# q and k brought in with their rows as columns, so that TensorE does not turn them

## The chip, the cores and the metric

The kernel runs on one core of one Trainium2 chip. Its time is the device time of one execution in microseconds (us); the median of several runs is compared. The profile shows one execution, engine by engine: PE is TensorE, PEld its weight loads, DVE is VectorE, ACT is ScalarE, POOL is GpSimd, and SPq is the queue of SyncE, which issues nearly all DMAs. What the host does to the inputs before the launch is not in this time.

## The reference, cut to what matters

```python
# q, k, v: (4 batches, 8 heads, 576 rows, 64), f32
scores = scale * np.matmul(q, k.transpose(0, 1, 3, 2))
thresh = np.max(scores, axis=-1, keepdims=True) - tau
scores = np.where(scores >= thresh, scores, -1000000000.0)
attn = softmax(scores)
x = attn @ v                     # then the heads side by side: 2304 x 512
x = np.maximum(x @ w_in, 0.0) ** 2 @ w_out          # 512 -> 2048 -> 512
# top-1 of 8 experts by x @ w_gate: relu(x @ w1[e]) @ w2[e], times two gates
```

## The kernel before

The work is a graph of tasks, each with an engine, a planned cost, the buffers that it reads and writes, and a key (a due time). `Graph.schedule` (L108) plays the graph through with the planned costs and fixes one order per engine; the program is written in that order, and every engine and the SP queue run theirs strictly in order. So the order comes from planned costs, and the times from the chip.

Attention goes by pairs of heads, 16 pairs (`pr`), four to a batch. A pair has 9 chunks of 128 query rows (`t_chunk`): scores on PE (L653; L688 for the first two chunks), row maximum on DVE (L656), threshold and exponential on ACT (L664, L659), masking with a sum on DVE (L668), normalizing on POOL or ACT (L679, L711), five transposes on PE (L733), copies out of PSUM on ACT (L744, L750) and DVE (L753), and then the product with v (`t_av`, L794 in the first batch, L776 later). While batch b is in attention, PE also does the first dense layer of batch b-1 (`t_h`, L873: 32 units of 12 matmuls for a batch). After the attention come the rest of that layer, the second layer (L991) and the experts (L1255, L1305).

Products keep f32 accuracy by splitting an operand into a rounded part (`hi`, type fp32r) and the rest (`lo`). Each pair is prepared during the pair before it (`pair_prep`):

- `t_load` brings k, q and v from HBM into `kraw`, `qraw`, `vraw`, one buffer each. For k and q, partition p gets rows 4p to 4p+3 of both heads in pieces of 64 numbers (256 bytes): a main DMA of 128x8x64 (L532) and a tail for the last 64 rows (L526).
- `t_qk` turns each of them, in two parts: 3 and 2 transposes on PE (L576) into a PSUM bank of the pool `pM`; then ACT makes `hi` from that bank (L584 for k, L586 for q, which is scaled through `qsc`) and DVE makes `lo` from the bank and `hi` (L592, L594). The results are `xk` and `xq`, with 2 x 64 channels of the two heads on the partitions and 576 rows as columns.
- `t_op` copies pieces of `xk` and `xq` within SBUF to the operands `opA` and `opB` of the scores (L608, L611, L614), and `t_diag` a piece of `xq` to `xd` (L629), on the SP queue.

The pool `pM` has two banks, and L576, the products with v and the units of `t_h` share them. `w_in` is fetched and converted during the attention too (`t_w`, DVE L850 to L854).

## Time and profile before

| | |
|---|---|
| median of 3 runs | 1034.44 us (1034.28 to 1034.68) |
| the profiled execution | 1033.64 us, its span from first to last instruction 1031.9 us |
| PE busy | 991.9 us, 96% of the span |
| PEld, DVE, ACT, POOL busy | 85%, 67%, 62%, 33% |
| DMA | 167.85 MB, of 165437 packets 60367 under 512 B |
| mean granted TensorE clock | 0.990 of full speed |

Busy shares are averages over stages with different limits, so the stages have to be read one by one. Matmuls are pipelined, and the busy time of a short group of them reaches past the start of the next instruction; the price of a group within a full stream is better read from its start to the next start. The difference of 1.7 us between the profiled execution and its span lies outside of the instructions.

### The profile page before, as it was taken

The page shows a single profiled execution, that of the slowest core. Times are in us where ns is not written, and L with a number is a line of the kernel's source. Part 1 is how long each engine was busy: PE and PEld are TensorE (multiplying, and loading weights), DVE is VectorE, ACT ScalarE, POOL GpSimd, SP SyncE. Part 2 cuts the span into 40 slices and gives each one's busy share as a digit, 9 for nine tenths or more (in the row PEclk, how much of TensorE's full clock was granted, in tenths as well). Part 3 has the DMA queues.
Part 4 walks back from the last instruction along what each step waited for, and adds up shares of the span by engine and source line. Part 5 has one row for each costly group of instructions (what it writes and reads, how often), then busy time and mean ns, then how long its engine had stood idle before and what let it go on. Part 6 is the DMA issues. An engine that isn't in the chain of part 4 may idle for free.

```text
span 1031.9 us, 19062 instructions
## 1 busy us (share of the span) xinstructions
PE 991.9 (96%) x6276; PEld 875.1 (85%) x6276; DVE 696.2 (67%) x1579; ACT 640.0 (62%) x1331; POOL 344.1 (33%) x660
## 2 busy tenths in 40 slices
PE   6999889999999999999999999999999999999995
PEld 5656589899999999999998888888889999889894
DVE  4668899987878778975972444434687667767730
ACT  5878667776666667765744444444666667867730
POOL 1234698775666566563000000010112211111200
PEclk9999989999999999999999999999999999999998
DMA  6556566654455544633882444433768868877700
GB/s 153 123 148 157 144 172 181 158 139 119 125 128 144 143 126 121 185 104 114 255 252 78 115 114 118 120 107 83 212 196 278 278 205 280 285 273 260 266 20 24
DMA packets 165437, 167.85 MB, mean 163 GB/s; under 512 B 60367, under 2 KB 126159, under 8 KB 165330
## 3 DMA queue, kind: packets, MB, share of 16 engines
q1 hardware_dynamic: 161090, 156.03, 52.8%
q0 software_dynamic: 4096, 10.52, 3.1%
q8 instruction: 52, 0.85, 0.3%
q14 instruction: 55, 0.45, 0.1%
q10 hardware_dynamic: 144, 0.00, 0.0%
HBM read 110.72 MB, written 29.56 MB: 136 GB/s over the span
## 4 chain that ended last, share of the span: by engine, by line
PE 74%; DVE 7%; issue 6%; DMA 6%; POOL 4%; ACT 2%; SPq 1%; DVEq 0%; POOLq 0%; ACTq 0%
PE bank L991 18%; PE bank L873 16%; PE bank L1305 8%; PE bank L1255 8%; PE bank L653 6%; PE bank L733 5%; PE bank L776 4%; PE bank L794 3%; DMA out_dram<-memf 2%; PE bank L1275 2%; DVE memf L656 2%; DVE memf L668 1%; PE bank L1110 1%; DVE memr L753 1%; POOL memf L679 1%
## 5 line engine op out<-in xcount | busy, mean ns | idle before, releaser
L873 PE MATMUL bank<-memr,w 128*128 128x288 f32 x1536 | 226.4, 298 | 1.5 <-DVE memr L594 1.4
L873 PEld LDWEIGHTS bank<-memr,w 128*128 128x128 f32 x1536 | 209.6, 189 | 3.6 <-DVE memr L594 3.2
L991 PE MATMUL bank<-w,memr 128*128 128x512 f32 x648 | 157.4, 394 | 0.0
L991 PEld LDWEIGHTS bank<-w,memr 128*128 128x128 f32 x648 | 119.1, 188 | 23.4
L668 DVE SCALAR_TENSOR_TENSOR memf<-bank,memf 128x576 f32<-128x576 f32 x144 | 116.0, 813 | 26.0 <-ACT memf L659 22.6
L656 DVE TENSOR_REDUCE memf<-bank 128x1 f32<-128x576 f32 x144 | 106.7, 750 | 23.5 <-PE bank L653 20.4
L653 PE MATMUL bank<-memr 128*128 128x288 f32 x600 | 110.9, 313 | 9.8 <-DVE memf L668 8.1
L733 PE MATMUL bank<-ident,memf 128*128 128x128 f32 x720 | 106.1, 278 | 9.2 <-ACT ptf L744 4.2
L679 POOL TENSOR_SCALAR memf<-memf 128x576 f32<-128x576 f32 x128 | 99.8, 782 | 31.2 <-DVE memf L676 21.3
L659 ACT ACTIVATE memf<-bank,memf 128x576 f32<-128x576 f32 x144 | 104.3, 732 | 0.0
L1096 POOL DMA_INDIRECT lst<-memf x18 | 17.8, 989 | 258.6 <-DVE memf L1082 112.8
L733 PEld LDWEIGHTS bank<-ident,memf 128*128 128x128 f32 x720 | 82.7, 142 | 21.1 <-issue 5.3
L653 PEld LDWEIGHTS bank<-memr 128*128 128x128 f32 x600 | 86.3, 192 | 15.5 <-DVE memf L668 11.1
L750 ACT ACTIVATE memr<-bank 128x640 fp32r<-128x640 f32 (+1 forms) x120 | 76.7, 649 | 25.6 <-PE bank L733 22.4
L1255 PE MATMUL bank<-memr,w 128*128 128x256 f32 x564 | 88.9, 283 | 0.7 <-DVE memr L1265 0.6
L976 DVE TENSOR_TENSOR memr<-memf,memr 128x512 fp32r<-128x512 f32 x72 | 48.3, 700 | 61.1 <-ACT memf L973 59.5
L1240 DVE TENSOR_TENSOR w<-memf,w 128x512 fp32r<-128x512 f32 x114 | 74.0, 687 | 16.0 <-ACT w L1237 12.5
L673 POOL TENSOR_SCALAR memf<-memf 128x1 f32<-128x1 f32 x144 | 31.2, 216 | 149.4 <-DVE memf L668 134.7
L753 DVE TENSOR_TENSOR memr<-bank,memr 128x512 fp32r<-128x512 f32 (+1 forms) x120 | 74.6, 629 | 9.2 <-ACT memr L750 7.7
L1255 PEld LDWEIGHTS bank<-memr,w 128*128 128x128 f32 x564 | 77.4, 191 | 2.0 <-DVE memr L1265 1.1
L1305 PE MATMUL bank<-memr 128*128 128x512 f32 x306 | 77.3, 393 | 0.0
L664 ACT ACTIVATE memf<-memf,ntau 128x1 f32<-128x1 f32 x144 | 41.5, 293 | 52.3 <-DVE memf L656 42.5
(145 smaller groups left out, 1743.8 us busy)
## 6 DMA issues: line engine op xcount, KB each, us to landing
memf<-in_moe_w_dram SPq DMA_DIRECT2D x104, 512.0 KB
r_scr<-memf SPq DMA_DIRECT2D x128, 144.0 KB
memf<-r_scr SPq DMA_DIRECT2D x36, 512.0 KB
memr<-memr SPq DMA_DIRECT2D x64, 144.0 KB
memr<-memr SPq DMA_DIRECT2D x64, 128.0 KB
memr<-memr SPq DMA_DIRECT2D x32, 256.0 KB
memf<-in_moe_w_in_dram SPq DMA_DIRECT2D x16, 512.0 KB
memf<-in_moe_w_out_dram SPq DMA_DIRECT2D x16, 512.0 KB
```

The source lines that it names most:

```text
L653: nc.tensor.matmul(s.t[:, hf, :HALF], qo, ko[:, halves[hf]], start=(i == 0), stop=(i == len(ops) - 1))
L656: nc.vector.tensor_reduce(nm.t, s.t[:, :, :HALF], axis=AX.XY, op=ALU.max, negate=True)
L659: nc.scalar.activation(p.t[:, :S].rearrange("p (a n) -> p a n", a=2), s.t[:, :, :HALF], AF.Exp, bias=nm.t)
L668: nc.vector.scalar_tensor_tensor(p3, s.t[:, :, :HALF], th.t, p3, op0=ALU.is_ge, op1=ALU.mult, accum_out=sm.t)
L679: nc.gpsimd.tensor_scalar(p.t[:, :S], p.t[:, :S], sm.t, 1.0, op0=ALU.mult, op1=ALU.mult)
L733: nc.tensor.transpose(ps.t[:, j], p.t[:, j * P : (j + 1) * P], ident)
L750: nc.scalar.activation(pt.t[:, :NQ, off : off + w], ps.t[:, :, c0 : c0 + w], AF.Copy)
L753: nc.vector.tensor_tensor(pt.t[:, NQ:, off : off + w], ps.t[:, : NQ - 1, c0 : c0 + w], pt.t[:, : NQ - 1, off : off + w].bitcast(F32), op=A ...
L873: nc.tensor.matmul(ps.t[:, :HALF], wv[:, a, kc], xT.t[:, x, kc, half], start=(i == 0), stop=(i == len(seq) - 1),)
L991: nc.tensor.matmul(ps.t, s.t[:, fc], wob[fc].t[:, x], start=(fc == 0 and i == 0), stop=(fc == NFC - 1 and i == 2))
L1255: nc.tensor.matmul(ps.t[:, :256], w1b[kc][fc // 4].t[:, a, (fc % 4) * P : (fc % 4 + 1) * P], x2.t[:, x, kc], start=(i == 0), stop=(i == 11))
L1305: nc.tensor.matmul(ps.t, hT.t[:, a, fc, u * P : (u + 1) * P], w2b[fc].t[:, x], start=(fc == 0 and i == 0), stop=(fc == 7 and i == 2))
```

## The change

`kernel()` lays q and k out on the host as (batch, pair, 2 x 64 channels, 576 rows), with the rows in the order in which the transposes left them. A load of k or q is then one DMA of 128 partitions x 2304 bytes, without a tail; `t_qk` has no PE task, takes no bank of `pM`, and makes `hi` and `lo` of all 576 columns by one ACT and one DVE instruction that read `kraw` or `qraw` in SBUF. Removed per pair: 10 transposes on PE, 2 of 4 instructions on ACT, 2 of 4 on DVE, 2 DMAs. A raw buffer, which became free after the transposes, becomes free after `lo`.

```diff
-        ("kraw", 1, [P, NQ, 2, D]), ("qraw", 1, [P, NQ, 2, D]), ("vraw", 1, [P, 2, NQ, D]),
+        ("kraw", 1, [P, S]), ("qraw", 1, [P, S]), ("vraw", 1, [P, 2, NQ, D]),
...
-        hs = {"k": k, "q": q, "v": v}[nm][b, 2 * hp : 2 * hp + 2]
+        if nm != "v":
+            src = {"k": k, "q": q}[nm][b, hp]
+            dma(lambda: nc.sync.dma_start(buf.t, src), P * S * 4, [], [buf], key)
+            return
...
-    def t_qk(pr, nm, part, key):
+    def t_qk(pr, nm, key):
...
-        def tp():
-            o = 0
-            for c in cs:
-                sz = QSZ[c]
-                nc.tensor.transpose(
-                    ps.t[:, o : o + sz], raw.t[:sz, c].rearrange("p a d -> p (a d)"), ident[:sz, :sz]
-                )
-                o += sz
...
-                nc.scalar.activation(X, ps.t[:, :n], AF.Copy, scale=qsc)
+                nc.scalar.activation(xy.t[:, 0], raw.t, AF.Copy, scale=qsc)
...
-                nc.vector.scalar_tensor_tensor(Y, ps.t[:, :n], qsc, X, op0=ALU.mult, op1=ALU.subtract)
...
-        g.add("PE", 0.109 * len(cs), tp, [(raw, 0), (raw, 1)] + ([(raw, 2)] if 4 in cs else []), [ps], key, hold=[xy])
-        g.add("ACT", c_act(n, True, nm == "q"), hi, [ps], [(xy, 0, part)], key - 1)
-        g.add("DVE", c_dve(n), lo, [ps, (xy, 0, part)], [(xy, 1, part)], key - 1)
+                nc.vector.scalar_tensor_tensor(xy.t[:, 1], raw.t, qsc, X, op0=ALU.mult, op1=ALU.subtract)
+
+        g.add("ACT", c_act(S, False, nm == "q"), hi, [raw], [(xy, 0)], key - 1)
+        g.add("DVE", c_dve(S), lo, [raw, (xy, 0)], [(xy, 1)], key - 1)
...
+    turned = {"k": order, "q": np.roll(order, 64)}
...
+        if name in turned:
+            a = np.swapaxes(a, 2, 3)[..., turned[name]].reshape(4, 4, 128, 576)
```

The order is planned anew. On PE, in the third batch, where pair 10 (counted from 0) is prepared during the chunks of pair 9, these rows stood before (bank_1_68 and bank_1_69 are the two banks of `pM`, bank_2_77 and bank_2_78 hold scores, w_80 and w_81 are parts of `w_in`):

```order
L776 MATMUL bank_1_68<-memr 128x320 x9
L576 MATMUL bank_1_69<-ident,memf 128x128 x3
L733 MATMUL bank_2_73<-ident,memf 128x128 x5
L653 MATMUL bank_2_78<-memr 128x288 x6
L576 MATMUL bank_1_68<-ident,memf 128x128
L576 MATMUL bank_1_68<-ident,memf 128x64
L576 MATMUL bank_1_69<-ident,memf 128x64
L576 MATMUL bank_1_69<-ident,memf 128x128 x2
L653 MATMUL bank_2_77<-memr 128x288 x4
L733 MATMUL bank_2_73<-ident,memf 128x128 x5
L576 MATMUL bank_1_68<-ident,memf 128x128 x2
L873 MATMUL bank_1_69<-memr,w_81 128x288 x12
```

In the changed kernel the same place on PE reads as follows, with new line numbers (L752 is the old L776, L629 the old L653, L709 the old L733, L849 the old L873):

```order
L752 MATMUL bank_1_68<-memr 128x320 x9
L629 MATMUL bank_2_78<-memr 128x288 x6
L709 MATMUL bank_2_73<-ident,memf 128x128 x5
L849 MATMUL bank_1_69<-memr,w_81 128x288 x12
L629 MATMUL bank_2_77<-memr 128x288 x4
L849 MATMUL bank_1_68<-memr,w_81 128x288 x4
L709 MATMUL bank_2_73<-ident,memf 128x128 x5
L849 MATMUL bank_1_68<-memr,w_81 128x288 x8
L752 MATMUL bank_1_69<-memr 128x256 x9
```

The ten transposes are gone, the units of `t_h` have moved up between the chunks, and nothing has come in the place of the transposes.

On the SP queue, at the start of the program, these rows stood before:

```order
L532 DMA memf<-in_k_dram 128x8x64
L526 DMA memf<-in_k_dram 64x2x64
L532 DMA memf<-in_q_dram 128x8x64
L526 DMA memf<-in_q_dram 64x2x64
L530 DMA memf<-in_v_dram 128x2x256
L524 DMA memf<-in_v_dram 64x2x64
L947 DMA lst<-memf 128x340
L532 DMA memf<-in_k_dram 128x8x64
L608 DMA memr<-memr 64x576 x2
L614 DMA memr<-memr 64x512
L611 DMA memr<-memr 64x2x512
L614 DMA memr<-memr 64x512
```

In the changed kernel the SP queue starts with these rows (L522 is the load of k or q, L584, L587 and L590 are the old L608, L611 and L614, L605 is the old L629):

```order
L522 DMA memf<-in_k_dram 128x576
L522 DMA memf<-in_q_dram 128x576
L530 DMA memf<-in_v_dram 128x2x256
L527 DMA memf<-in_v_dram 64x2x64
L923 DMA lst<-memf 128x340
L927 DMA y_scr<-memf 1x513
L584 DMA memr<-memr 64x576 x3
L587 DMA memr<-memr 64x2x512
L590 DMA memr<-memr 64x512 x2
L584 DMA memr<-memr 64x576
```

The load of q is now the second DMA instead of the third, and the next pair's load of k no longer stands ahead of the first pair's copies; it follows behind all of them.

## Rows read from the trace of the kernel before

**Rows 1.** Busy time by stage: PE, PEld, DVE, ACT, POOL, then clock, DMA share, GB/s.

```profile
15.00:105.00 90.00, 80.91 (x453) 55.38 (x453) 65.76 (x152) 72.18 (x149) 29.26 (x56) 1.00 0.59 142
105.00:190.00 85.00, 77.85 (x500) 66.14 (x500) 75.93 (x167) 60.12 (x128) 64.66 (x119) 0.94 0.59 156
190.00:427.00 237.00, 234.33 (x1789) 226.94 (x1788) 193.53 (x441) 163.37 (x358) 151.21 (x340) 1.00 0.54 139
427.00:960.00 533.00, 531.95 (x3149) 468.24 (x3148) 332.66 (x767) 314.05 (x637) 88.15 (x124) 1.00 0.60 186
```

**Rows 2.** Busy time by stage, L576 alone: PE, PEld, clock, DMA share, GB/s.

```profile
0.00:15.00 15.00, 3.69 (x13) 2.28 (x13) 1.00 0.75 176
15.00:105.00 90.00, 7.71 (x42) 4.98 (x42) 1.00 0.59 142
105.00:190.00 85.00, 4.56 (x23) 2.74 (x23) 0.94 0.59 156
190.00:568.00 378.00, 15.07 (x82) 9.89 (x82) 1.00 0.54 148
```

**Rows 3.** Timeline of PE from 278.1 us: start, duration, instruction, idle before.

```profile
278.16 0.49 PE L576 MATMUL bank<-ident,memf 128*128 128x128 f32 x3
278.48 0.71 PE L733 MATMUL bank<-ident,memf 128*128 128x128 f32 x5
...
279.83 0.90 PE L576 MATMUL bank<-ident,memf 128*128 128x128 f32 x5
280.49 0.77 PE L653 MATMUL bank<-memr 128*128 128x288 f32 x4
...
281.65 0.38 PE L576 MATMUL bank<-ident,memf 128*128 128x128 f32 x2
282.24 0.40 PE L873 MATMUL bank<-memr,w 128*128 128x288 f32 x1 [0.21 <-DVE memr L594]
...
307.71 0.49 PE L576 MATMUL bank<-ident,memf 128*128 128x128 f32 x3
```

**Rows 4.** Groups by line: xcount, busy us, mean ns, idle before.

```profile
L594 DVE SCALAR_TENSOR_TENSOR memr<-bank,qsc,memr 128x320 fp32r<-128x320 f32 (+1 forms) x32 | 16.3, 511 | 1.5 <-ACT memr L586 1.4
L586 ACT ACTIVATE memr<-bank,qsc 128x320 fp32r<-128x320 f32 (+1 forms) x32 | 15.7, 500 | 2.7 <-PE bank L576 1.5 <-DVE memf L668 0.4 <-DMA memf<-in_moe_w_out_dram 0.2
L592 DVE TENSOR_TENSOR memr<-bank,memr 128x384 fp32r<-128x384 f32 (+1 forms) x32 | 14.2, 451 | 3.0 <-ACT memr L584 2.5
L584 ACT ACTIVATE memr<-bank 128x384 fp32r<-128x384 f32 (+1 forms) x32 | 13.0, 414 | 8.6 <-PE bank L576 7.7 <-DVE memr L592 0.7
L711 ACT ACTIVATE memf<-memf 128x576 f32<-128x576 f32 x16 | 12.2, 779 | 0.4 <-DVE memf L676 0.4
L976 DVE TENSOR_TENSOR memr<-memf,memr 128x512 fp32r<-128x512 f32 x72 | 48.3, 700 | 61.1 <-ACT memf L973 59.5 <-DMA memf<-in_moe_w_dram 1.6
```

**Rows 5.** Chain that ended last, first 16 us: start, duration, what.

```profile
0.73 3.98 DMA memf<-in_k_dram
...
6.90 0.99 PE bank L576 x3
...
8.48 0.95 DVE memr L594 x2
...
9.45 0.62 SPq L611
...
10.12 4.83 DMA memr<-memr
```

**Rows 6.** Waits of the SP queue: us in total, times, longest.

```profile
SPq L532 <- PE bank L576: 35.9, 15, 6.0
```

**Rows 7.** Line L576, PE's idle time before it by releaser: us, times.

```profile
  DMA memf<-in_k_dram: 4.9, 1
```

**Rows 8.** Busy time by stretch, columns as in Rows 1.

```profile
103.00:112.00 9.00, 6.39 (x28) 4.47 (x28) 8.16 (x18) 5.96 (x13) 5.53 (x9) 0.81 0.53 136
130.00:139.00 9.00, 5.79 (x28) 4.49 (x28) 8.96 (x20) 5.84 (x14) 8.76 (x15) 0.75 0.65 168
```

More of the change, by code (lines that the diff above doesn't have):

```diff
@@ L555, in t_v @@
             g.add("POOL", 0.1 + NQ * D * 0.0024, lo, src + [(buf, j, 0)], [(buf, j, 1)], key)
-    def t_qk(pr, nm, part, key):
+    def t_qk(pr, nm, key):
         raw = raws[pr, nm]
-        xs = xks if nm == "k" else xqs
-        if pr not in xs:
-            xs[pr] = new("x" + nm, pr)
-        xy = xs[pr]
-        if nm == "k":
-            cs, n0 = ((0, 1, 2), 0) if part == 0 else ((3, 4), 384)
-        else:
-            cs, n0 = ((4, 0, 1), 0) if part == 0 else ((2, 3), 320)
-        n = sum(QSZ[c] for c in cs)
-        ps = Buf(pM, f"tp{pr}{nm}{part}")
-        def tp():
-            o = 0
-            for c in cs:
-                sz = QSZ[c]
-                nc.tensor.transpose(
-                    ps.t[:, o : o + sz], raw.t[:sz, c].rearrange("p a d -> p (a d)"), ident[:sz, :sz]
-                )
-                o += sz
+        xy = (xks if nm == "k" else xqs)[pr] = new("x" + nm, pr)
         def hi():
-            X = xy.t[:, 0, n0 : n0 + n]
             if nm == "k":
-                nc.scalar.activation(X, ps.t[:, :n], AF.Copy)
+                nc.scalar.activation(xy.t[:, 0], raw.t, AF.Copy)
             else:
-                nc.scalar.activation(X, ps.t[:, :n], AF.Copy, scale=qsc)
+                nc.scalar.activation(xy.t[:, 0], raw.t, AF.Copy, scale=qsc)
         def lo():
-            X = xy.t[:, 0, n0 : n0 + n].bitcast(F32)
-            Y = xy.t[:, 1, n0 : n0 + n]
+            X = xy.t[:, 0].bitcast(F32)
             if nm == "k":
-                nc.vector.tensor_tensor(Y, ps.t[:, :n], X, op=ALU.subtract)
+                nc.vector.tensor_tensor(xy.t[:, 1], raw.t, X, op=ALU.subtract)
             else:
-                nc.vector.scalar_tensor_tensor(Y, ps.t[:, :n], qsc, X, op0=ALU.mult, op1=ALU.subtract)
-        g.add("PE", 0.109 * len(cs), tp, [(raw, 0), (raw, 1)] + ([(raw, 2)] if 4 in cs else []), [ps], key, hold=[xy])
-        g.add("ACT", c_act(n, True, nm == "q"), hi, [ps], [(xy, 0, part)], key - 1)
-        g.add("DVE", c_dve(n), lo, [ps, (xy, 0, part)], [(xy, 1, part)], key - 1)
+                nc.vector.scalar_tensor_tensor(xy.t[:, 1], raw.t, qsc, X, op0=ALU.mult, op1=ALU.subtract)
+        g.add("ACT", c_act(S, False, nm == "q"), hi, [raw], [(xy, 0)], key - 1)
+        g.add("DVE", c_dve(S), lo, [raw, (xy, 0)], [(xy, 1)], key - 1)
     def t_op(pr, j, key):
@@ L614, in turn_q @@
             nc.sync.dma_start(q3(slice(64, 128))[:, 1 - x], xq.t[rows, x, 64:].bitcast(F32))
-        parts = lambda xy, *xs: [(xy, x, p) for x in xs for p in range(2)]
+        parts = lambda xy, *xs: [(xy, x) for x in xs]
         for x in range(2):
@@ L629, in t_diag @@
             dma(lambda r=r: nc.sync.dma_start(xd.t[r, :, r].bitcast(F32), xq.t[r, :, 0:64].bitcast(F32)),
-                32768, [(xq, x, 0) for x in range(2)], [(xd, j)], key)
+                32768, [(xq, x) for x in range(2)], [(xd, j)], key)
     def t_chunk(n, key):
@@ L692, in mm @@
                     i += 1
-            rd = [(xk, x, p) for x in range(2) for p in range(2)] + [(xq, x, 0 if c < 2 else 1) for x in range(2)]
+            rd = [(y, x) for y in (xk, xq) for x in range(2)]
             g.add("PE", c_pe(HALF) * 8, mm, rd, [s], key)
         elif hd == 2:
-            rd = [(xk, x, p) for x in range(2) for p in range(2)] + [(xds[pr], j) for j in range(2)]
+            rd = [(xk, x) for x in range(2)] + [(xds[pr], j) for j in range(2)]
             g.add("PE", c_pe(HALF) * 6, mm, rd, [s], key + K("scores", pr))
@@ L1324, in pair_prep @@
         for nm in "kq":
-            for part in range(2):
-                t_qk(pr, nm, part, key)
+            t_qk(pr, nm, key)
         for j in range(2):
@@ L1423, in put @@
         args.append(nc.dram_tensor(name, a.shape, mybir.dt.from_np(a.dtype), kind="ExternalInput").ap())
+    p = np.arange(512)
+    order = np.concatenate([4 * (p % 128) + p // 128, np.arange(512, 576)])
+    turned = {"k": order, "q": np.roll(order, 64)}
     for name in _INS:
-        a = np.ascontiguousarray(inputs[name])
+        a = inputs[name]
+        if name in turned:
+            a = np.swapaxes(a, 2, 3)[..., turned[name]].reshape(4, 4, 128, 576)
+        a = np.ascontiguousarray(a)
         if a.ndim == 0:
```

13 lines of the change are left out of this document (4 added, 9 removed).

## The prediction

> **What bounds the kernel now.** PE is by far the busiest engine of the page (96% of the span, the table above), so the first question is in which stages its work is what time is made of. The busy times by stage [rows 1] tell. From 190 us on PE is full: 234.33 of 237 us while attention runs beside the first dense layer, and 531.95 of 533 after that. DVE, the next engine, has 193.53 of the 237, so PE alone sets the pace there, and what PE does not do is saved one for one. Before 190 us it is different. From 15 to 105 us (the first batch, no dense work beside it) PE has 80.91 of 90 and ACT 72.18: mostly PE, with pauses for the chain of a chunk. From 105 to 190 us DVE has 75.93 of 85, PE 77.85, and the granted clock is 0.94: two engines close to full, and neither covers the other.
>
> Then I read L576, the transposes of q and k, alone by stage [rows 2]: 13 before 15 us, 42, 23, and 82 from 190 us on, together the 160 of 16 pairs. Last, the timeline of PE in the full stretch [rows 3], for the price of one preparation; there a preparation comes every 307.71 - 278.16 = 29.55 us.
>
> **The change part by part.**
>
> *Transposes from 190 us on.* The busy times of L576 [rows 2] reach past the start of the next instruction, so I price a preparation from start to next start [rows 3]: 278.48 - 278.16 = 0.32, 280.49 - 279.83 = 0.66, 282.24 - 281.65 = 0.59, together 1.57 us for ten transposes. The last holds a wait of 0.21 us for DVE, which frees the bank of `pM`; it goes too, since q and k take no bank any more. 82 transposes are 8.2 preparations: 8.2 x 1.57 = 12.9 us. Nothing comes in their place on PE, as the order shows. I take all of it, because PE is full before and after; the lower bound is 10, if every preparation leaves a new pause of about 0.35 us.
>
> *Transposes from 15 to 105 us.* 42 of them, at most 4.2 x 1.57 = 6.6 us; nothing, if the chain of a chunk sets the pace throughout. PE's 90% is nearer to the first, but some transposes also fill pauses: I take 4.0.
>
> *From 105 to 190 us.* 23 transposes, at most 3.6 us. Here DVE counts as much as PE, so its saving is worked out. The makers of `lo` cost (16.3 + 14.2) / 16 = 1.91 us per pair now, those of `hi` on ACT (15.7 + 13.0) / 16 = 1.79 [rows 4]. The new ones read SBUF, and q and k have no such row. Nearest on ACT is L711, 576 columns out of SBUF with a scale, 779 ns; nearest on DVE is L976, 512 columns out of SBUF, 700 ns, so 788 for 576. Two each make 1.56 on ACT and 1.58 on DVE, 0.23 and 0.33 less per pair. (Were one instruction as dear as the two that it replaces, the difference would be nothing.) Three pairs in this stretch give DVE 1.0 us. With a little of the PE work I take 1.5, between 0 and 3.6. From 190 us on the savings of ACT and DVE are worth nothing, because PE's work covers them.
>
> *The start.* The chain of the first 16 us [rows 5] runs: load of k (from 0.73, 3.98 long), transposes and parts of k, transposes of q (6.90), `lo` of q ready at 8.48 + 0.95 = 9.43, copies to the operands, the last of which lands at 10.12 + 4.83 = 14.95, scores. In the changed kernel the load of q is SP's second DMA, issued one issue time (some 0.65, from 9.45 to 10.12) after the first, at 1.4. If it takes the 3.98 of k, q is there at 5.4; `hi` takes 0.78, `lo` 0.79, ready at 7.0 instead of 9.43: 2.4 us. The copies behind it are as many and as large, and the next pair's load of k no longer runs beside them. Bounds: 1.0, if the loads get in each other's way and q lands 1.4 later; 4, if loads in rows of 2304 bytes are shorter by 1.6. No row of this kernel shows q or k loaded in whole rows.
>
> The Trainium skill, DMA: Bandwidth & Descriptors, Specifications, puts the smallest transfer at line rate at 512 B; the pieces grow from 256 to 2304 bytes, so by it the load shortens, the start gives up to 4 us, and the total would be 1012.0 instead of the 1013.6 below.
>
> *DMA and SP.* 32 DMAs fewer on the SP queue I count as nothing, since PE has no idle time in the full stretch that they could end. A raw buffer becomes free after `lo` instead of after the transposes, 9.43 - 7.89 = 1.5 us later for q [rows 5]. The next load waits for the buffer on SP already: 35.9 us in 15 waits [rows 6], so it is issued as soon as the buffer is free, most of the 29.55 us of a pair ahead of its use, and 1.5 us of these cost nothing. Behind the waiting load stand, on SP, the copies of the same pair, which need `lo` themselves. Were a load needed at once, the 1.5 us would be paid by ACT (the last rival).
>
> Sum: 12.9 + 4.0 + 1.5 + 2.4 = 20.8 us. The profiled execution took 1033.64, which gives 1012.8; the median of the runs shown is 0.8 above it, so I forecast **1013.6 us**.
>
> **The rivals.**
>
> *Only the full stretch and part of the start pay.* Before 190 us the chain of a chunk over DVE, ACT and POOL sets the pace, and PE just pauses longer. For it: DVE's 75.93 of 85 and ACT's 72.18 of 90 [rows 1]. Against: PE is above 89% in both stages. Gain 12.9 + 1.0 = 13.9: 1020.5 us.
>
> *More than the sum.* PE's work before 190 us is saved in full, and the clock no longer falls there, because the units of `t_h` move up into the pauses (in the new order 84 instead of 40 of its matmuls stand ahead of the end of the fifth pair's transposes of chunks). The trace has two stretches of 9 us at 0.81 and 0.75 of the clock [rows 8], so 38% and 50% of the time at 1.2 instead of 2.4 GHz: 7.9 us that do the work of 4. Gain 12.9 + 6.6 + 3.6 + 2.4 + 4.0 = 29.5: 1004.9 us.
>
> *The clock falls oftener.* PE is busy 6.39 and 5.79 of 9 us where the clock is 0.81 and 0.75 [rows 8], so pauses and the lower level come together, and less work on PE means more pauses before 190 us. A stretch like the second has 4.5 us at half speed and loses 2.25 us of work. One more for each of the pairs 1 to 6 loses 13.5: 1027.1 us; it would take nine to eat the gain. Against: from 15 to 105 us the clock stays at 1.00 although PE pauses 10% of the time [rows 1].
>
> The Trainium skill, TensorE: Matmul & The Clock Gate, Part 1, says that half rate is the default and that activity lifts it, which speaks for this rival; the trace agrees so far that the lower level stands where PE pauses most [rows 8].
>
> *Slower: ACT waits for the loads.* Before, a late load held up only PE's transposes; now `hi` itself waits for it, in ACT's order, and behind it stand the exponentials and the copies out of PSUM for which PE waits. It decides from 20.8 / 32 = 0.65 us per load that passes through to PE; at 1 us for each of the 32 loads the time is 1013.6 + 32 = 1045.6 us. Against: PE waited for a load of k once, 4.9 us at the start, and never again [rows 7], and the loads are issued most of a pair ahead.
>
> **How the numbers follow.** The forecast gets 0.56, with 1009 to 1018 as its own range; more than the sum 0.15; only the full stretch 0.20; the clock 0.05; the wait for loads 0.04. The range reaches over the two large neighbours: 1004 (the 29.5 of the larger case and a little of the start's upper bound) to 1024 (the lower bounds, 10 + 0 + 0 + 1.0 = 11.0, give 1023.4). A measurement of this kernel can tell about 0.2%, 2 us, from no change. All cases but the last end far below 1032; the last gives slower its 0.04, and 0.02 stays for a tie between it and the others, taken from the clock's.
>
> **What would show it.** Right: no transposes of q and k on PE; PE above 98% from the seventh pair to 960 us; a preparation every 28.0 instead of 29.55 us; the first copies landed near 12.5 instead of 14.95 us; one `hi` near 0.78 and one `lo` near 0.79 us. Wrong: ACT idle before `hi` until a load of q or k lands; new PE pauses of over 0.3 us per pair in the full stretch; a clock below 0.94 in the second batch; the first batch as long as before.

## The result and the profile after

The changed kernel takes **1019.3 us** (median of 4 runs, 1017.7 to 1021.6) where the kernel before takes 1034.4 beside it: ratio 0.9855, 95% interval 0.9843 to 0.9866. The forecast was 1013.6 us; the time lies in the range of 1004 to 1024, but 1.3 us outside of the likeliest case's own range, and 1.2 us from the rival "only the full stretch and part of the start pay" (1020.5). So the direction and the main mechanism held, and some 6 of the 20.8 us did not come. The profiled execution is the slowest of the four, 1021.6 us with a span of 1019.8; it is 12.0 us shorter than the profiled one of before.

The times of the four go with the mean granted TensorE clock of their spans: 1021.6 us at 0.992, 1019.3 at 0.994 and 0.995, 1017.7 at 0.996. In the profiled one the lower level stands twice before 190 us, with PE busy throughout (columns as in [rows 1]):

```profile
88.60:92.00 3.40, 3.40 (x9) 1.61 (x8) 3.19 (x8) 2.76 (x6) 0.62 (x2) 0.50 0.67 192
129.60:132.90 3.30, 3.30 (x16) 3.30 (x16) 2.29 (x5) 0.93 (x2) 3.22 (x6) 0.50 0.53 172
```

That is 6.8 us at half speed, so at most 3.4 us lost. A few us between two profiles can be the clock's, and the clock has to be read beside every mark below. In the kernel before, the lower level stands 10.2 us before 190 us (0.94 over 85 us, [rows 1]).

Busy time by stage in the changed kernel (columns as in [rows 1]):

```profile
15.00:105.00 90.00, 77.93 (x414) 51.29 (x413) 63.21 (x143) 71.24 (x141) 30.01 (x56) 0.98 0.54 139
105.00:190.00 85.00, 77.33 (x518) 66.86 (x518) 75.72 (x162) 62.51 (x128) 67.27 (x121) 0.98 0.64 171
190.00:427.00 237.00, 229.90 (x1757) 223.84 (x1757) 200.56 (x441) 166.39 (x354) 167.57 (x353) 1.00 0.53 139
427.00:960.00 533.00, 530.59 (x3115) 465.64 (x3114) 333.92 (x765) 316.23 (x639) 83.39 (x111) 1.00 0.62 190
```

Read against [rows 1]: from 15 to 105 us PE does 3 us less and just pauses 3 us more. From 105 to 190 DVE is as full as before, POOL 2.6 us fuller. And from 190 to 427 PE is no longer full, 229.90 instead of 234.33 of 237: the full stretch now begins near 240 us. The 50 us ahead of that, before and then changed:

```profile
190.00:240.00 50.00, 48.53 (x366) 46.01 (x365) 43.33 (x95) 35.29 (x78) 37.72 (x72) 1.00 0.62 160
```

```profile
190.00:240.00 50.00, 44.78 (x329) 41.90 (x329) 45.04 (x93) 34.41 (x74) 40.53 (x71) 1.00 0.59 157
```

The most telling number is in no view as a row; it is put together from the timelines of two engines. On DVE, the row maximum (L656 before, L632 now) of a pair's first chunk tells when the pair starts. On PE, the matmuls of `t_h` ahead of that moment, divided by 12, tell how many units the dense layer has had, since a pair that starts early only because units were put off has gained nothing. (Pairs are counted from one here. A unit takes some 1.6 us of PE in the full stretch.)

| us from the span's start | before | changed |
|---|---|---|
| fifth pair | 113.0 (0 units) | 113.0 (0 units) |
| ninth pair | 238.3 (25.3) | 237.3 (27.0) |
| tenth pair | 269.2 (34.0) | 263.9 (34.0) |
| last of the 144 chunks | 471.62 (88.8) | 457.85 (88.8) |

In this profile the first batch has gained nothing. At the ninth pair the lead is 1.0 us and 1.7 units more. At the tenth pair, with equal units, it is 5.3 us, and the six preparations that follow add 8.4, that is 1.40 each. After the attention 1.8 of the 13.8 us are lost again in this pair of profiles; that part of the program is the same in both, and over the kernels below that end with the same work it took 559.5 to 563.6 us (560.3 and 562.0 here), so the 1.8 us say nothing of the change.

The new instructions, by line (xcount, busy us, mean ns, idle before):

```profile
L569 DVE TENSOR_TENSOR memr<-memf,memr 128x576 fp32r<-128x576 f32 x16 | 14.3, 892 | 1.2 <-ACT memr L562 1.2
L571 DVE SCALAR_TENSOR_TENSOR memr<-memf,qsc,memr 128x576 fp32r<-128x576 f32 x16 | 13.7, 856 | 0.7 <-ACT memr L564 0.4
L564 ACT ACTIVATE memr<-memf,qsc 128x576 fp32r<-128x576 f32 x16 | 12.3, 769 | 0.8 <-issue 0.6 <-DMA memf<-in_q_dram 0.2
L562 ACT ACTIVATE memr<-memf 128x576 fp32r<-128x576 f32 x16 | 10.9, 678 | 2.9 <-DMA memf<-in_k_dram 2.7
```

ACT's 0.68 and 0.77 us are what was assumed or less. DVE's 0.89 and 0.86 are more than the 0.79. Where the excess comes from is seen in the timeline of DVE and POOL at 214 us (start, duration, engine, instruction):

```profile
214.66 1.30 POOL L834 TENSOR_TENSOR w<-memf,w 128x512 fp32r<-128x512 f32 x1
214.69 0.08 DVE L644 DVE_READ_ACCUMULATOR memf<-bank,memf 128x1 f32 x1
214.69 1.88 DVE L569 TENSOR_TENSOR memr<-memf,memr 128x576 fp32r<-128x576 f32 x1
216.04 0.58 POOL L649 TENSOR_SCALAR memf<-memf 128x1 f32<-128x1 f32 x1
```

`lo` of k begins beside POOL's subtraction for `w_in`, takes 1.88 us and ends 0.61 after POOL has ended; then POOL's operation on one column, 0.19 us elsewhere, ends with `lo`. The old `lo` of k read a bank of PSUM and took 0.45 for each of its two parts [rows 4].

PE's longest waits between 105 and 240 us (us in total, times, longest):

```profile
PE bank L709 <- DVE memr L729: 4.2, 5, 1.7
PE bank L709 <- DVE memf L652: 2.3, 4, 1.1
PE bank L629 <- DVE memf L644: 1.7, 4, 0.9
```

All three are waits for DVE: the turn of the probabilities (L709) waits for a bank that DVE empties or for the reciprocal of a sum, the scores (L629) for the mask. Behind them stand two of 1.5 us for ACT. In the first batch it is ACT for which PE waits, 9.4 us where it was 4.2: for its copies of the turned probabilities out of PSUM (L720, before L744), ahead of the next turn (L709, before L733) and of the product with v (L770). From 15 to 105 us, changed and then before:

```profile
PE bank L709 <- ACT ptf L720: 7.1, 5, 2.5
PE bank L770 <- ACT ptf L720: 2.3, 3, 0.9
```

```profile
PE bank L733 <- ACT ptf L744: 4.2, 5, 1.2
```

So the theory to be tested was **A**: from the fifth pair to the ninth, VectorE (with GpSimd beside it, and the conversion of `w_in` on both) sets the pace, and takes up what PE is spared. The main rival, **B**: the newly planned order costs the missing us.

### The profile page after: what moved, and what is told of

It is laid out like the page before. It is cut to its first block, busy times and chain, and to the rows that moved or that the text cites. A ratio compares the mean times of both kernels' runs of the same rounds, so it can differ in the third digit from the quotient of the medians.

```text
span 1019.8 us, 18567 instructions
## 1 busy us (share of the span) xinstructions
PE 969.8 (95%) x6116; PEld 856.1 (84%) x6116; DVE 692.5 (68%) x1547; ACT 636.4 (62%) x1299; POOL 357.8 (35%) x660
## 4 chain that ended last, share of the span: by engine, by line
PE 65%; DVE 11%; issue 7%; DMA 6%; POOL 5%; ACT 5%; SPq 0%; POOLq 0%; DVEq 0%; ACTq 0%
PE bank L967 18%; PE bank L849 12%; PE bank L1281 8%; PE bank L1231 8%; PE bank L709 4%; PE bank L629 4%; PE bank L770 3%; DVE memf L644 3%; DMA out_dram<-memf 3%; DVE memf L632 3%; PE bank L752 3%; ACT memf L635 2%; DVE memr L729 2%; DMA memf<-in_moe_w_dram 1%; PE bank L1086 1%
## 5 line engine op out<-in xcount | busy, mean ns | idle before, releaser
L849 PE MATMUL bank<-memr,w 128*128 128x288 f32 x1536 | 228.2, 297 | 0.7 <-POOL memr L793 0.5
L849 PEld LDWEIGHTS bank<-memr,w 128*128 128x128 f32 x1536 | 210.4, 188 | 1.4 <-POOL memr L793 0.8
L709 PE MATMUL bank<-ident,memf 128*128 128x128 f32 x720 | 105.9, 278 | 20.2 <-ACT ptf L720 8.6
L632 DVE TENSOR_REDUCE memf<-bank 128x1 f32<-128x576 f32 x144 | 106.1, 748 | 19.0 <-PE bank L629 15.8
L629 PE MATMUL bank<-memr 128*128 128x288 f32 x600 | 110.8, 314 | 3.7 <-DVE memf L644 3.7
L709 PEld LDWEIGHTS bank<-ident,memf 128*128 128x128 f32 x720 | 81.1, 141 | 37.1 <-issue 9.8
L1072 POOL DMA_INDIRECT lst<-memf x18 | 18.5, 1026 | 257.4 <-DVE memf L1058 193.9
L629 PEld LDWEIGHTS bank<-memr 128*128 128x128 f32 x600 | 87.0, 194 | 8.8 <-DVE memf L644 6.9
L729 DVE TENSOR_TENSOR memr<-bank,memr 128x512 fp32r<-128x512 f32 (+1 forms) x120 | 74.9, 630 | 8.4 <-ACT memr L726 7.1
L649 POOL TENSOR_SCALAR memf<-memf 128x1 f32<-128x1 f32 x144 | 37.1, 258 | 115.3 <-DVE memf L644 103.7
```

The costliest lines, as they stand in the source:

```text
L629: nc.tensor.matmul(s.t[:, hf, :HALF], qo, ko[:, halves[hf]], start=(i == 0), stop=(i == len(ops) - 1))
L632: nc.vector.tensor_reduce(nm.t, s.t[:, :, :HALF], axis=AX.XY, op=ALU.max, negate=True)
L709: nc.tensor.transpose(ps.t[:, j], p.t[:, j * P : (j + 1) * P], ident)
L729: nc.vector.tensor_tensor(pt.t[:, NQ:, off : off + w], ps.t[:, : NQ - 1, c0 : c0 + w], pt.t[:, : NQ - 1, off : off + w].bitcast(F32), op=A ...
L849: nc.tensor.matmul(ps.t[:, :HALF], wv[:, a, kc], xT.t[:, x, kc, half], start=(i == 0), stop=(i == len(seq) - 1),)
```

## The experiments

The times are compared with the kernel before on the same chip. Pair starts are worked out as above, each from one profiled execution. At the tenth pair every kernel has had 34.0 units.

| run | time, us (ratio, 95%) | fifth | ninth (units) | tenth | last chunk |
|---|---|---|---|---|---|
| same order | 1192.6 | 124.0 | 252.1 (25.3) | 283.0 | 488.5 |
| transposes kept | 1028.4 (0.991 to 0.996) | 111.1 | 234.5 (25.3) | 265.0 | 464.0 |
| last two batches | 1026.0 (0.989 to 0.993) | 114.1 | 238.2 (25.3) | 268.0 | 462.0 |
| first batch | 1036.2 (0.9995 to 1.002) | 108.0 | 238.2 (25.3) | 268.9 | 471.4 |
| same order, mended | 1044.5 (1.009 to 1.013) | 112.9 | 244.6 (25.3) | 275.6 | 480.6 |
| changed, light bits | not compared | 110.0 | 224.8 (27.0) | 251.7 | 445.7 |
| before, light bits | not compared | 110.2 | 229.6 (25.3) | 260.5 | 463.0 |
| changed, conversions 6 chunks earlier | 1018.8 (0.984 to 0.987) | 110.6 | 231.3 (25.3) | 260.6 | 455.0 |
| changed, 12 chunks earlier | 1018.5 (0.983 to 0.986) | 117.6 | 232.5 (25.2) | 262.1 | 455.2 |
| before, 12 chunks earlier | 1035.7 (1.000 to 1.002) | 116.2 | 240.3 (25.3) | 270.9 | 473.4 |
| changed, sum without GpSimd | 1010.1 (0.973 to 0.978) | 113.6 | 227.0 (25.7) | 256.7 | 448.5 |

### The old order, twice

In the kernel before, with the new layout, the PE task of `t_qk` stays in the plan but issues nothing, and the whole `hi` and `lo` stand where the first part stood:

```diff
         def tp():
-            o = 0
-            for c in cs:
...
+            pass
```

> The changed work, written in the order that was planned for the kernel before: its 160 transposes are simply left out, hi and lo of all 576 columns stand where the halves of part 0 stood, and the tails stand for nothing. Theory A (transposes before about 230 us filled pauses that stay, and DVE sets the pace there): the new plan is not the cause, 1019 us within 3 us. Rival B (the new planned order costs the missing 6 us, above all in the first batch and in pairs 6 to 8): near the forecast, 1012 to 1015 us.

The edit was flawed: the plan frees the raw buffer after the empty task, so nothing keeps the next load from overwriting it before `lo` has read it. `lo` then works on another pair's numbers and the experts get other tokens, so the total says nothing. The attention, whose instructions don't depend on the numbers, can be read: its last chunk starts at 488.5 us, 16.9 later than in the kernel before. In the mended kernel `hi` and `lo` hold the buffer:

```diff
-        g.add("DVE", c_dve(n), lo, [ps, (xy, 0, part)], [(xy, 1, part)], key - 1)
+        rd = [(raw, x) for x in range(3)]
+        g.add("DVE", c_dve(n), lo, [ps, (xy, 0, part)] + rd, [(xy, 1, part)], key - 1)
```

> The change's layout and its whole-row parts, but the planner still books the 64 transposes, their bank and their two parts (the transposes are then not issued), and the parts hold the loaded buffer until they are done, so that the other instructions of TensorE stand nearly in the order of before (6627 of 7067 in the same sequence). Theory A (from the fourth pair to the eighth VectorE, with GpSimd beside it, sets the pace and takes up what TensorE is spared there; the new order is innocent): 1017 to 1023 us, the ninth pair starts at 236 to 239 us as in both kernels (238.3 and 237.3), and each later pair takes 28.0 to 28.3 us. Rival B (the order that the planner found for the changed kernel costs the missing 5 us, and the old order would have kept them): 1011 to 1016 us, the ninth pair starts at 231 to 234 us.

1044.5 us, slower than before, which neither theory had. PE's waits between 190 and 427 us in this kernel show where it goes (L728 is the turn of the probabilities, L748 the `lo` of the probabilities out of PSUM):

```profile
PE bank L728 <- DVE memr L748: 13.4, 10, 2.8
```

PE waits 1.3 us a time; in the changed kernel the same wait (L709 for L729) is 4.2 us between 105 and 240 us (above) and 0.3 from there to 427. Why is argued from the order, and not tested by itself: a `hi` and a `lo` of 576 columns stand at places where the plan had shorter ones, and push the work behind them. The lower clock level also stands longer ahead of the last chunk, some 20 us against 6.8 in the changed kernel (in the first of these two runs some 30). So the old order doesn't keep the gain, it costs some 25 us against the new one; but it was planned for other work, and that the new order loses something at single places (rival B) is not excluded by it.

### What a preparation's 1.5 us consist of

The changed kernel with ten transposes per pair put back, whose results nobody reads; `hi` and `lo` still come from SBUF:

```diff
+                        nc.tensor.transpose(ps.t[:sz, i * P : (i + 1) * P], raw.t[:, QOFF[c] : QOFF[c] + sz], ident)
...
+                g.add("PE", 0.109 * len(cs), tp, whole, [ps], key, hold=[xy])
```

> The changed kernel, but PE still makes the 10 transposes per pair, from kraw and qraw into a bank of pM that nobody reads; hi and lo are made from SBUF as in the change. Theory A (PE work after about 230 us is what was saved): the time returns to 1030 to 1034 us, only the 2 us of the start stay gained. Rival C (whole-row loads, one instruction instead of two on ACT and DVE and fewer DMAs give the gain): it stays near 1019 us.

1028.4 us: faster than expected, and faster than before with as many transposes. At the tenth pair it is already 4.3 us ahead of the kernel before, where the changed kernel is 5.3 ahead; its lower clock level stands as long as in the changed kernel, 6.8 us (at 78 and 129 us). So up to there the transposes' own work was worth 1.1 us, and the rest of the lead came with the rest of the change, the new order and a shorter time at the lower level included. From the tenth pair to the last chunk it gains 3.4 us on the kernel before, 0.56 for each of the six preparations, and the changed kernel gains 5.0 on it, 0.84 each. Its timeline of PE (the transposes are L580):

```profile
302.66 0.49 PE L580 MATMUL bank<-ident,memf 128*128 128x128 f32 x3
302.99 0.71 PE L774 MATMUL bank<-ident,memf 128*128 128x128 f32 x5
303.53 0.38 PE L580 MATMUL bank<-ident,memf 128*128 128x128 f32 x2
303.67 1.04 PE L694 MATMUL bank<-memr 128*128 128x288 f32 x6
304.55 0.71 PE L580 MATMUL bank<-ident,memf 128*64 128x128 f32 x5
305.02 0.76 PE L694 MATMUL bank<-memr 128*128 128x288 f32 x4
```

Read as in [rows 3], from start to next start: 0.33 + 0.14 + 0.47 = 0.94 us for ten, where the kernel before needs 1.57. So of a preparation's price some 0.9 us are the transposes themselves. The other 0.6 went with what this kernel lacks too: the hand-over of `pM` to ACT and DVE in four parts (0.21 of it is the wait in [rows 3]), in the new layout and order; the run doesn't tell these apart. Taking only the transposes' own work would have priced the change too low.

### The change in two batches, or in the first alone

Both layouts are passed in, and a pair goes the new way where `direct(pr)` says so; pairs 9 to 16 in one kernel, 1 to 4 in the other.

```diff
+    def direct(pr):
+        return pr in range(8, 16)      # the other kernel: range(4)
```

> Only pairs 8 to 15 take the new way (both layouts of q and k are inputs); pairs 0 to 7 keep their transposes. Theory A: these 8 preparations lie where PE is full, 8 x 1.57 = 12.6 us less, 1021 to 1023 us, so nearly the whole gain of the change. Rival D (in the late stretch new pauses eat a third, as the gain of 8.2 us from chunk 63 to chunk 144 could be read): 1026 us.

> Only pairs 0 to 3 take the new way. Theory A: the start gives some 2 us and the other three pairs nothing, because their transposes stood in pauses: 1031.5 to 1033 us. The step as forecast (start 2.4 and 4.0 from 15 to 105 us): 1028 us.

With pairs 9 to 16 alone the kernel takes 1026.0 us (1023.2 to 1027.4) and gains 8.4: not the 1021 to 1023 of theory A but the 1026 of rival D. At its last chunk it leads by 9.7 us, of which 1.2 were there at the tenth pair's start: the full stretch pays, 1.40 us for each of the six preparations instead of 1.57. With pairs 1 to 4 alone it gains nothing (1036.2, neither the 1031.5 to 1033 of theory A nor the 1028 as forecast), and yet its fifth pair starts some 5 us early, 108.0 instead of 113.0, with the lower level ahead of it as long in both. At the seventh pair it is 1.3 us later with one unit more (174.2 against 172.9 us), at the ninth, with equal units, level (238.2 against 238.3). So what PE is spared in the first batch can be had, and is taken away again in the second.

### VectorE relieved in both kernels

Two of DVE's three bit operations for each slice of `w_in` are not issued, and the third takes one operand; plan and order stay. The sign and the last bits of `w_in` are left out, and with them the routing of tokens changes, so only the attention is compared.

```diff
-        g.add("DVE", c_dve(512, 2), lambda: ts(si(), ai(), -2147483648, None, op0=ALU.bitwise_and), [av], [sg], key)
+        g.add("DVE", c_dve(512, 2), lambda: i < NFC or ts(si(), ai(), -2147483648, None, op0=ALU.bitwise_and), [av], [sg], key)
...
+              lambda: ts(ai(), ai(), 3, None, op0=ALU.logical_shift_left) if i < NFC
```

> The changed kernel, with two of VectorE's three bit operations on each of the 16 slices of w_in not issued and the third with one operand (sign and last bits of w_in are left out, so the first feed-forward and the routing that follows it work on other numbers; what comes after attention isn't compared). The order is that of the changed kernel. That takes 1.4 to 1.7 us from VectorE per slice, some 20 us of its 212 busy between 15 and 427 us minus what lies elsewhere. Theory A (VectorE sets the pace there): the start of the ninth pair, 237.3 us in the changed kernel, falls to 226 to 232 us, and the lead over the kernel before with the same edit is 4 to 8 us instead of 1.0. Rival B (order): it falls by the same amount in both kernels, lead 0 to 2 us. Rival C (TensorE's own chain of score, turn, part sets the pace there): it falls by under 2 us in either.

> The kernel before with the same two bit operations per slice of w_in not issued and the third with one operand (sign and last bits of w_in are left out), in its own order. Theory A: VectorE is not what holds it here once it is relieved, TensorE with its transposes is: the start of the ninth pair, 238.3 us, falls by 3 to 6 us, to 232 to 235 us, less than in the changed kernel. Rival B: it falls as far as in the changed kernel. Rival C: it falls by under 2 us.

The ninth pair starts 12.5 us earlier in the changed kernel, 8.8 in the kernel before; the lead there goes from 1.0 to 4.8 us, at the tenth pair from 5.3 to 8.8, at the last chunk from 13.8 to 17.3. Both kernels fell further than theory A had it (12.5 for about 5 to 11, 8.8 for 3 to 6), and the units are the same with and without the edit. The stretch from 105 to 190 us in the changed kernel, and then in the kernel before, both with light bits (columns as in [rows 1]):

```profile
105.00:190.00 85.00, 80.35 (x560) 71.07 (x561) 69.22 (x156) 65.67 (x135) 66.73 (x130) 1.00 0.70 186
```

```profile
105.00:190.00 85.00, 81.72 (x546) 71.33 (x545) 65.64 (x154) 63.93 (x137) 61.34 (x125) 0.95 0.65 169
```

With DVE at 69 of 85 instead of 75.7, PE gets through 560 matmuls there instead of 518. So DVE's work does hold back this stretch in both kernels, and rival C (no fall) is out.

That DVE hides 3.5 us of what the change saves, as the growth of the lead could be read, is not shown, because the clock differs too. From 80 to 145 us, in the changed kernel, the changed one with light bits, the kernel before, and that one with light bits (columns as in [rows 1]):

```profile
80.00:145.00 65.00, 56.84 (x323) 41.58 (x324) 52.52 (x112) 47.95 (x97) 43.85 (x68) 0.95 0.59 158
80.00:145.00 65.00, 58.47 (x362) 44.50 (x361) 47.16 (x107) 52.33 (x105) 44.62 (x79) 1.00 0.64 169
80.00:145.00 65.00, 57.40 (x309) 40.35 (x308) 55.10 (x117) 47.88 (x101) 40.60 (x66) 0.92 0.64 161
80.00:145.00 65.00, 60.10 (x329) 43.45 (x329) 44.32 (x110) 49.51 (x104) 40.25 (x74) 0.92 0.66 168
```

In the kernel before, the light bits leave the clock as it was. In the changed one neither of its two stretches at the lower level is there with them, 6.8 us that cost up to 3.4, as much as the lead grows. Without this part the fall at the ninth pair would be an estimated 9.1 us (12.5 - 3.4) against 8.8, which is rival B (equal fall in both). Nor must the clock have risen because DVE was relieved: the changed kernel with its conversions 6 chunks earlier, below, keeps 1.00 there too, with DVE's work whole. At the fifth pair the two kernels with light bits stand level, 110.0 and 110.2, so the first batch's loss is not DVE's work on `w_in`.

### VectorE beside GpSimd, by itself

No attention at all: three DVE instructions, each alone and then beside three POOL instructions.

> No attention at all (zeros are written out): three VectorE instructions, the subtraction from SBUF 128x576, the subtraction from PSUM 128x512 and the bit operation from SBUF 128x512, each alone, then beside GpSimd's subtraction of two SBUF operands 128x512, its scaling of one 128x576, and its 128x1 operation. Theory A (VectorE and GpSimd lengthen each other where both read two operands from SBUF): the subtraction from SBUF takes 0.75 us alone and 1.1 to 1.9 beside GpSimd's subtraction, the bit operation 0.68 alone and 0.9 to 1.3; the one from PSUM stays within 10% of its time alone; GpSimd's 128x1 operation goes from 0.19 to about 0.57 us beside the two from SBUF and stays near 0.19 beside the one from PSUM. Rival D (the long ones in the trace are waits that the profile shows as busy time): every instruction stays within 10% of its time alone.

Groups by line in windows of this kernel. The subtraction from SBUF (L32) alone, then beside POOL's subtraction (L41), its scaling (L44) and its one column (L47):

```profile
L32 DVE TENSOR_TENSOR vlo<-vraw,vhi 128x576 fp32r<-128x576 f32 x16 | 12.1, 758 | 0.5
...
L32 DVE TENSOR_TENSOR vlo<-vraw,vhi 128x576 fp32r<-128x576 f32 x16 | 27.3, 1709 | 0.5
L41 POOL TENSOR_TENSOR glo<-graw,ghi 128x512 fp32r<-128x512 f32 x16 | 26.1, 1631 | 1.2
...
L32 DVE TENSOR_TENSOR vlo<-vraw,vhi 128x576 fp32r<-128x576 f32 x22 | 24.3, 1106 | 0.8
L44 POOL TENSOR_SCALAR gs<-graw 128x576 f32<-128x576 f32 x23 | 23.8, 1034 | 1.8
...
L32 DVE TENSOR_TENSOR vlo<-vraw,vhi 128x576 fp32r<-128x576 f32 x21 | 15.9, 758 | 0.7
L47 POOL TENSOR_SCALAR g<-g 128x1 f32<-128x1 f32 x21 | 14.9, 711 | 1.7
```

And the subtraction from PSUM (L35) beside POOL's subtraction, then POOL's three alone:

```profile
L35 DVE TENSOR_TENSOR vlo<-bank,vhi 128x512 fp32r<-128x512 f32 x21 | 14.5, 691 | 0.7
...
L41 POOL TENSOR_TENSOR glo<-graw,ghi 128x512 fp32r<-128x512 f32 x16 | 20.2, 1262 | 1.2
...
L44 POOL TENSOR_SCALAR gs<-graw 128x576 f32<-128x576 f32 x15 | 10.1, 671 | 1.2
...
L47 POOL TENSOR_SCALAR g<-g 128x1 f32<-128x1 f32 x15 | 2.9, 191 | 1.2
```

The long times are real, and rival D falls. With two operands in SBUF, DVE goes from 0.758 to 1.709 us beside POOL's subtraction and to 1.106 beside its scaling; this last was not expected. The bit operation goes the same way, 0.693 to 1.574 and 1.018. Beside one column DVE keeps its 0.758, and POOL's 0.191 becomes 0.711. With one operand in PSUM nothing changes on either side (0.691).

The Trainium skill, SBUF — State Buffer, "SBUF: two separate sides", says that a VectorE instruction with two SBUF inputs and a GpSimd instruction that reads SBUF exclude one another, the later one being blocked for the whole of the earlier. The trace agrees on which instructions do it. By whole exclusion the two subtractions would come every 0.758 + 1.262 = 2.02 us; they come 1.7 apart, so some 0.3 us of them do overlap.

In the changed kernel this costs DVE, between 105 and 235 us, 5 x (1.20 - 0.75) = 2.3 us for `lo` of k and 12 x (0.22 + 0.15) = 4.4 us for the two long bit operations, whose mean there is 0.93 and 0.86 us, against 0.70 each in the slices converted from 427 us on, where no POOL subtraction for `w_in` runs. The bit operations suffered already before the change (0.84 and 0.79 there); `lo` is new in it, because it used to read PSUM.

### The conversions moved earlier

```diff
-    W1, W2 = 60, 8.0
-    W0 = 34
+    W1, W2 = 42, 8.0      # 12 chunks: 24
+    W0 = 28               # 12 chunks: 22
```

> The changed kernel with the loads and conversions of w_in planned 6 chunks (some 18 us) earlier, nothing else. Theory A (VectorE's work on w_in, 2.25 us a slice, is what sets the pace from 105 to 235 us; VectorE has 27 us free between 15 and 105): about two slices more are converted ahead of 105 us, the ninth pair starts 2 to 4.5 us earlier, at 233 to 235.5 us instead of 237.3, and the total falls to 1015 to 1018 us. Rival E (before 105 us ScalarE and the chain of a chunk have no room for the 1.3 us that a slice takes of ScalarE): the fifth pair starts 2 to 4 us later than 113 us and the total stays at 1018 to 1023 us.

> The changed kernel with the loads and conversions of w_in planned 12 chunks (some 36 us) earlier. Theory A: about five slices more ahead of 105 us, 11 us of VectorE's work, of which 5 to 9 us come off the start of the ninth pair (228 to 232 us instead of 237.3); total 1010 to 1015 us. Rival E: the fifth pair starts 4 to 8 us later and the total stays at 1017 us or above.

> The kernel before, with its transposes, and the same 12 chunks: what the earlier conversions are worth without the change. Theory A: the stretch is held by VectorE only as far as TensorE with its transposes leaves it (relieved by two bit operations a slice, this kernel's ninth pair started 8.7 us earlier, the changed one's 18.2 us): 2 to 5 us, total 1029 to 1033 us. Rival F (the earlier conversions are worth the same to both kernels, and have nothing to do with the change): the same gain as in the changed kernel, within 1 us.

(The changed kernel's ninth pair started 12.5 us earlier with light bits, not 18.2.) Theory A overrated this. By 6 chunks DVE takes 6.1 us more ahead of 105 us (69.31 instead of 63.21), and the fifth pair is not late (110.6); the ninth starts 6.0 us earlier with 1.7 units fewer, the last chunk 2.9 us earlier. But the granted clock is 1.00 in both early stages of this profile, which is worth up to 3.4 us of that, and the total of 1018.8 us is the changed kernel's. Neither theory had this. By 12 chunks, with 6.8 us at the lower level as in the changed kernel, the ninth pair starts 4.8 us earlier with 1.8 units fewer, the tenth only 1.8, and the total of 1018.5 us is within the intervals of the changed kernel's. The stretches from 15 to 190 us in it (columns as in [rows 1]):

```profile
15.00:105.00 90.00, 74.14 (x394) 48.94 (x393) 70.56 (x147) 72.38 (x143) 36.16 (x57) 0.98 0.61 164
105.00:190.00 85.00, 76.30 (x496) 62.80 (x496) 78.66 (x164) 62.84 (x128) 66.93 (x119) 0.98 0.57 156
```

DVE takes 7.4 us more ahead of 105 us, PE gets 3.8 us less done, and the fifth pair starts 4.7 us late: rival E, for the larger step alone. That DVE's free time in the first batch lies inside the chain of a chunk, and is not all free for long instructions, is argued from this. The kernel before gains nothing either.

### A wait of VectorE taken away

The sum of a row goes from DVE's mask to POOL, which adds 1e-9, and back to DVE's reciprocal. Without POOL's part (the addition of 1e-9 is left out):

```diff
-        g.add("POOL", 0.16, r1, [], [sm], key + K("sum", pr))
```

> The changed kernel without GpSimd's 128x1 operation between VectorE's mask and VectorE's reciprocal (the addition of 1e-9 to the sum of a row is left out; a row's sum holds a 1 for its maximum, and beside it 1e-9 lies below the last place). Between 105 and 235 us VectorE stood 4.6 us idle for that operation, which takes 0.33 us there on average, and GpSimd spent 12.5 us in it. Theory A (VectorE sets the pace from 105 to 235 us): those 4.6 us and a part of GpSimd's come off that stretch, nothing off the full one after it: the ninth pair starts 3 to 6 us earlier (231 to 234 us instead of 237.3), total 1013 to 1017 us. Rival G (VectorE's share there is high but what the stretch waits for is TensorE's and ScalarE's chain in the planned order): the ninth pair starts within 2 us of 237.3, total 1017 to 1022 us.

1010.1 us (1006.9 to 1013.1), ratio 0.9756 with 0.9731 to 0.9781: faster than both kernels, and by more than expected. The ninth pair starts 10.3 us earlier, with 1.3 units fewer; the tenth 7.2 earlier, the last chunk 9.4. It is not the clock: the lower level stands 10.2 us in this profile, 6.8 in the changed kernel's. The reciprocal (here L649) between 105 and 235 us, and the stretch:

```profile
L649 DVE RECIPROCAL memf<-memf 128x1 f32<-128x1 f32 x42 | 6.3, 153 | 0.1
```

```profile
105.00:190.00 85.00, 79.37 (x551) 70.72 (x551) 80.55 (x177) 66.20 (x138) 66.64 (x103) 0.98 0.68 185
```

In the changed kernel DVE stands idle 5.5 us before 38 reciprocals there, 4.6 of it until POOL's column is done; here 0.1 before 42. DVE is busy 80.55 of 85 instead of 75.72 and PE gets 551 matmuls done instead of 518. So DVE's chain does hold back this stretch. What the edit would give the kernel before was not tried, so this gain is beside the change, and not a part of it; that DVE takes up what the change spares PE is not shown by it.

## Why the prediction was right, and where it was too high

**The full stretch (12.9 us): right, a little high.** 1.40 us per preparation from the tenth pair on, instead of 1.57, so 11.5 for 8.2 of them, inside the bounds of 10 and 12.9; the pairs come every 28.1 us, where 28.0 were expected. PE's share of over 98% was expected from the seventh pair on; it is reached from about 240 us (188.12 of 190 from 240 to 430), and 190 to 427 as a whole has 97%. That some 0.6 us of each preparation is not the transposes' own work was in the start-to-start price of [rows 3] without being told apart there.

**The start, the first batch, the second batch (2.4 + 4.0 + 1.5 = 7.9 us): these terms were too high.** At the tenth pair 2.2 x 1.57 + 7.9 = 11.3 us should have been there, and 5.3 were. If the 2.2 preparations between 190 us and that mark are put at 1.40 too, 13.8 - 11.5 = 2.3 us are left for the three terms. The kernel that kept its transposes led by 4.3 us there, so the transposes' own work on PE, from which the 4.0 and a third of the 1.5 were priced, paid 1.1 up to that mark.

*The start* came as a chain and did not last. Timeline of the changed kernel's first 13 us:

```profile
0.73 0.41 SPq L522 DMA_DIRECT2D memf<-in_k_dram  x1
1.20 0.44 SPq L522 DMA_DIRECT2D memf<-in_q_dram  x1
5.18 0.68 ACT L562 ACTIVATE memr<-memf 128x576 fp32r<-128x576 f32 x1 [2.73 <-DMA memf<-in_k_dram]
6.05 0.78 ACT L564 ACTIVATE memr<-memf,qsc 128x576 fp32r<-128x576 f32 x1 [0.18 <-DMA memf<-in_q_dram]
6.86 0.82 DVE L571 SCALAR_TENSOR_TENSOR memr<-memf,qsc,memr 128x576 fp32r<-128x576 f32 x1 [0.20 <-ACT memr L564]
12.67 2.41 PE L629 MATMUL bank<-memr 128*128 128x288 f32 x8 [1.59 <-DVE memf L644]
```

The load of q is issued at 1.20, and ACT can take it at 6.0 instead of the 5.4 assumed; `lo` of q is ready at 7.68 instead of 9.43 (forecast 7.0), and the third chunk's scores start at 12.67, by then held up by DVE and not by a copy. Before, they started at 15.08:

```profile
15.08 2.26 PE L653 MATMUL bank<-memr 128*128 128x288 f32 x8 [1.54 <-DMA memr<-memr]
```

These are the 2.4 us. But the fifth pair starts at 113.0 us in both kernels, and "the first batch as long as before" was one of the signs of a wrong forecast. The loads did not get shorter with their longer rows: ACT takes k 4.45 us after the start of its issue, where the transfer was 3.98 long [rows 5]. (q is now issued 0.5 us behind k, before it was 1.6, and what the two cost each other is not told apart.) The Trainium skill, DMA: Bandwidth & Descriptors, Specifications, puts the smallest transfer at line rate at 512 B; the shorter load that the prediction worked out from it is not in this trace.

*The first batch* gave nothing in this profile: the lower bound, 0, was the right one. PE's busy time falls by 3.0 us and its pauses grow by as much; its waits for ACT's copies grow from 4.2 to 9.4. It isn't the clock: the lower level stands as long ahead of the fifth pair in both kernels (3.4 us, at 88.6 and at 107.2 us), though the changed kernel with its conversions 6 chunks earlier, which has none there, starts that pair at 110.6, so an execution without it may do better than this one. With only the first four pairs changed, some 5 us did arrive at the fifth pair, so the time isn't gone by necessity; which place of the changed kernel's order loses it is not settled. DVE's bit operations are not it (both kernels with light bits stand level there).

*The second batch*: the step that failed is "DVE counts as much as PE, so its saving is worked out", with 0.33 us less DVE per pair. The price of `lo` was taken from L976, an instruction at a time when POOL is nearly idle; beside POOL's conversions it measured 0.89 and 0.86 instead of 0.79 us on average and up to 1.88. Two such per pair make 1.75 us, 0.16 instead of 0.33 less than before; between 105 and 235 us they are 1.20 and 0.83, together 0.11 more than before. So the new `lo` spares DVE nothing there, and DVE's chain holds back the stretch: relieving it moved the ninth pair by 8.8 us in the kernel before and by an estimated 9.1 in the changed one. Whether DVE is also what kept the saving on PE (23 transposes, 3.6 us) from showing stays open, since the clock accounts for as much as the lead grew once DVE was relieved.

**The rivals.** "Only the full stretch" was right in its mechanism for the stages before 190 us, PE just pausing longer: DVE's 75.93 of 85 and ACT's 72.18 of 90 were the rows that spoke for it, and 0.20 was too little. "More than the sum" and "the clock falls oftener" are both out: the clock is 0.98 in both early stages, down from 1.00 and up from 0.94, so 6.8 us at the lower level instead of 10.2. (The 7.9 us that the prediction read in [rows 8] are too few: the second window ends at 139 us, the lower level at 141.3.) The fastest of the four executions, 1017.7 us, had a mean clock of 0.996, so 1.6 of the missing 5.7 us go with the clock, which the sum did not hold. "ACT waits for the loads" is out: ACT waited for k 2.7 us and for q 0.2, each once, at the start.

## What to carry to other kernels

Work taken off the busiest engine paid nearly in full (1.40 of 1.57 us per preparation) where it alone was full. In the stages where it shared the load with DVE or ACT, some 2 of 7.9 us came, as worked out above: price such a saving near its lower bound, and look first for idle time of the other engine inside its own chain (here a wait for a one-column operation of POOL, worth 9 us). An instruction that is moved from PSUM to SBUF operands has to be priced beside what GpSimd does at that time, not by a row from a quiet stage. A lead at one mark counts only with equal side work done and an equal clock: two stretches at the lower level, 6.8 us that cost up to 3.4, were as large here as the effect that was looked for. And an order planned for other durations is no control: the kernel with the old order lost some 25 us against the new one.

## What the runs showed of the hardware

DVE with two SBUF operands and POOL reading SBUF lengthen each other: 0.758 and 1.262 us alone become 1.71 and 1.63, while a subtraction of 512 columns from PSUM stays at 0.691. A POOL operation on one column, 0.191 us alone, takes 0.711 beside such DVE instructions; it stood 144 times in a chain between two DVE instructions.

The lower clock level still showed twice in the changed kernel, from 88.6 to 92.0 and from 129.6 to 133.0 us. Busy times by stretch:

```profile
85.00:95.00 10.00, 7.54 (x34) 4.41 (x32) 7.66 (x18) 7.51 (x15) 3.09 (x5) 0.83 0.64 160
...
121.00:130.00 9.00, 7.51 (x44) 5.46 (x42) 8.17 (x20) 6.58 (x14) 7.31 (x11) 0.98 0.64 165
130.00:139.00 9.00, 9.00 (x60) 8.66 (x59) 6.49 (x15) 4.40 (x10) 8.76 (x17) 0.84 0.47 128
```

The second one stands in a stretch where PE is busy throughout (at half speed, 1.2 instead of 2.4 GHz, for a part of it) and follows one where it paused 1.5 of 9 us. In [rows 8] the lower level stood in windows where PE paused most; here, at both places, PE is busy all the while that it stands, and the pauses come before it. Other executions of the same kernel had less of it (0.996 instead of 0.992 over the span).
